# State and conversion words through PSUM, a first slice on VectorE, and a clip folded into a product, in a one-core attention and MLP kernel

## The chip, the cores and the metric

One NeuronCore of a Trainium2 chip runs the whole program. The metric is device time in microseconds (us). The time of a kernel is the median of its runs; one further execution was profiled, and it has a time of its own.

## The reference

For each of 4 batches and 8 heads a linear recurrence with complex decay runs over 768 steps (head width 48); its output goes through a 2D Fourier mix, a normalised MLP, a token mixer and a second MLP:

```python
scale = minimum(mag, 0.999) / (mag + 1e-06)       # mag = |a|
S_re, S_im = ar*S_re - ai*S_im + k v^T, ar*S_im + ai*S_re   # each step
y[t] = q[t] @ S_re
X = fft(fft(x, axis=1), axis=2); u = x + real(X)
un = (u - mean) / sqrt(var + 1e-06)
x = u + relu(un @ w_ch1) @ w_ch2                  # 384 -> 1536 -> 384
u = x + (relu(x^T @ w_tok1) @ w_tok2)^T           # 768 -> 256 -> 768
out = u + relu(u @ w3) @ w4
```

The inputs are float32, and so is the output. The weights arrive as 64-bit words.

## The kernel before, in words

Each batch has a chain part (VectorE, ScalarE, GpSimd, some TensorE) and a dense part (mostly TensorE). The chain of batch 0 runs alone; then the chain of batch b+1 runs beside the dense part of batch b, and the last batch's dense part runs with the one before it.

**The chain.** The 96-step chunks of all heads are scanned at once on 128 partitions: 49 steps, grouped in slices of 4 (batch 0, `first_scan`, L314) or of 3 (`scan`, L553). A slice is prepared by short stages: `st_b` (L357: Square on ScalarE, sum on GpSimd), `st_c` (L369: Ln, Exp, Square on ScalarE, a product on GpSimd), `st_d`, `st_e1`, `st_e2` (L379 to L401: limited magnitude, then the tile `A` of factors on VectorE and GpSimd). `st_f` (L403) does one step with three dependent VectorE instructions into the PSUM tile `P`. Beside each slice of `first_scan`, `st_s` squares the products and forms a reciprocal on ScalarE and GpSimd, `st_r` and `st_x` (L454, L458) scale the keys by it, `st_y` multiplies keys and queries, and `st_t` transposes them on TensorE. In `scan` the inverse length is a third row of `P`, limited to `R_CAP` at L625 once a slice.

`stage1` (L719) then walks over 8 chunks. `ch_u` (L788) forms keys times values on TensorE, adds the state `T` (L804), multiplies by gates (L810 to L812, the last of them on GpSimd) and writes the next `T` (L814); `ch_sc` masks the scores (L785) and `ch_y` forms the outputs. `stage2` (L986) does the Fourier mix and the normalisation.

**The conversions.** `convert` (L180) turns one block of 64-bit weights into a pair of float32 parts, 56 blocks in all, through a tile `cvt`: load, ScalarE `L191` (high words, scaled, absolute) and `L192` (low words), VectorE shift `L194`, GpSimd add `L196`, VectorE sign merge `L199`, ScalarE cast `L205`, GpSimd difference `L206`, store. Twenty blocks are converted during batch 0's chain (`tick`, `feed`); the other 36 (`lead`, L242) during batch 0's dense part, each shortly before its use, and ahead of the chain in VectorE's order.

**The dense part.** `mlp` (L939) runs groups of nine products per PSUM bank (L952, L974); ScalarE and VectorE split the hidden activations (L956, L965), and VectorE adds results (L977).

**Order.** Each instruction has a priority by stream (`RANK`, L60): TensorE takes the chain first, VectorE, ScalarE and GpSimd take dense work first, conversions second, chain third. A planner places the instructions of each engine in a fixed order from these priorities and its own estimates; `vq` in `first_scan` fixes VectorE's order by hand. PSUM has eight banks, handed out by `palloc` (L101) in rotation under three names: `s` 3, `l` 3, `p` 2.

Of the kernel before, what the change touches and what calls it, by code (L numbers as in the profile page):

```python
# [31 lines left out]
WC = (0, 0, 0, 0, 0, 0, 10, 12)  # L32
WZ, CL = 0, 1
XL = (0,), (0, 1, 2, 3, 4, 5)
# [19 lines left out]
def attn_fft_mixer_kernel(ctx: ExitStack, tc: tile.TileContext, aL, xL, vL, wL, qN, kN, vN, arN, aiN,  # L54
# [124 lines left out]

    def convert(p, j, w=None, held=True):  # L180

# [8 lines left out]
        lo, hi, a = raw[:, :, 0], raw[:, :, 1], t[:, 2 * n:3 * n]  # L190
        se.activation(out=a.bitcast(F32), in_=hi.bitcast(F32), func=ACTF.Abs, scale=2.0 ** -112)  # L191
# [25 lines left out]
    def begin():  # L217
        p, j = convs.pop(0)
        return convert(p, j, ws.place if (p, j) in early else None)

# [21 lines left out]
    def lead():  # L242

        keep, stream[0] = stream[0], BACK
        while len(begun) < 3 and later:
            p, j = later.pop(0)
            g = convert(p, j, ws.place, len(later) > 32)
# [66 lines left out]
    def first_scan(t, knd, qk):  # L314
# [42 lines left out]
        def st_b(i):  # L357
# [6 lines left out]
            if i >= AH:  # L364
                after(x, t[i - AH]["scan"])
            ge.tensor_tensor(out=tm[:, 0, :].rearrange("p (a c) -> p a c", c=48), in0=sq[:, :, 0, :], in1=sq[:, :, 1, :], op=ALU.add)  # L366
            d["tm"] = tm

        def st_c(i):  # L369
# [4 lines left out]

            se.activation(out=tt, in_=r0, func=ACTF.Square, accum_out=low[:, i:i + 1])
            ge.tensor_tensor(out=tt, in0=x, in1=tt, op=ALU.mult)

# [14 lines left out]
        def st_e2(i):  # L392
            d = t[i]
            n = d["n"]
            A = with_ap(alloc(turns("A", ("A", "T")), [128, 4, 192], name="A"), 0, [(192, n), (48, 4), (1, 48)])
            vq(ve.tensor_tensor(out=A[:, :, 2:4, :], in0=d["raw"], in1=d["c1"].unsqueeze(2).to_broadcast([128, n, 2, 48]), op=ALU.mult))
            ge.tensor_tensor(out=A[:, :, 0:2, :], in0=with_ap(A[:, 0, 3, :], 0, [(192, n), (0, 2), (1, 48)]),
                             in1=with_ap(both, 0, [(0, n), (1, 2), (0, 48)]), op=ALU.mult)
            d["A"] = A
            P = palloc("l" if i % 3 == 2 else "p", [128, N4, 96])  # L400
            d["P"] = P[:, 0:n, :].rearrange("p n (c f) -> p n c f", c=2)  # L401

        def st_f(i, j, between=()):  # L403
# [3 lines left out]
            if s == 0:  # L407
                se.copy(out=P[64:128, 0, 0, :], in_=A[64:128, 0, 2, :])
                se.copy(out=P[64:128, 0, 1, :], in_=A[64:128, 0, 1, :])
                ve.memset(P[0:64, 0, 0, :], 1.0)  # L410
                ve.memset(P[0:64, 0, 1, :], 0.0)
                for f in between:
                    f()
                return
# [99 lines left out]
        def line_up(i):  # L514
# [38 lines left out]
    def scan(b, t, knd, qk):  # L553
# [57 lines left out]
        def st_f(i, j):  # L611
# [20 lines left out]
        def st_g(i):  # L632
# [86 lines left out]
    def stage1(b):  # L719
# [68 lines left out]
        def ch_u(c):  # L788
            d = st[c]
            ps = palloc(PU, [112, 8, 48])  # L790
            for h in range(8):
                vv = d["v"][:, h * 48:h * 48 + 48]
                te.matmul(out=ps[0:64, h, :], lhsT=d["kt"][:, h, 0:64], rhs=vv)  # L793
                te.matmul(out=ps[64:112, h, :], lhsT=d["kt"][:, h, 64:112], rhs=vv)
            g = gm[b % 2].rearrange("p k (h c) -> p k h c", c=8)[:, :, :, c:c + 1]
# [16 lines left out]
            st["yop"] = (ge if c else ve).tensor_tensor(out=v8(y)[64:112], in0=a[0:48], in1=gb(1, 0, 48), op=ALU.mult)  # L812
            T = alloc("e", [112, 384], name="T")
# [566 lines left out]
```

## Time and profile before

| | |
|---|---|
| time, median of 3 runs (lowest, highest) | 1082.09 us (1080.92, 1084.59) |
| profiled execution: own time, span | 1079.18 us, 1077.4 us |
| TensorE, VectorE, ScalarE, GpSimd busy, share of the span | 91%, 72%, 48%, 39% |
| mean granted TensorE clock | 0.967 |

The span is the stretch that the trace covers; the execution's own time is 1.8 us more. An engine counts as busy while one of its instructions runs, also while that instruction is held up inside. A matmul that was issued behind another overlaps it, so the duration of one is longer than its spacing. PE is TensorE, DVE VectorE, ACT ScalarE, POOL GpSimd. A granted clock of 1.00 is 2.4 GHz.

### The profile page before, as it was taken

What the parts mean: (1) busy time and instruction counts of PE and PEld (TensorE: products, weight loads), DVE (VectorE), ACT (ScalarE), POOL (GpSimd) and SP (SyncE); (2) the same over time, 40 slices, a digit from 0 to 9 for tenths busy, and PEclk for the clock granted to TensorE, in tenths of its full rate; (3) what the DMA queues carried; (4) which work ended last, traced back from release to release, by engine and by line L of the source; (5) the groups of instructions that cost most, each with busy time, mean ns of one, the idle gap of its engine ahead of it and who ended that gap; (6) DMA issues with size and microseconds to landing.
All of it is one profiled execution on the core that took longest, in us unless ns stands there. A gap on an engine that the chain in (4) does not pass through costs nothing.

```text
span 1077.4 us, 21129 instructions
## 1 busy us (share of the span) xinstructions
PE 979.0 (91%) x7314; PEld 915.2 (85%) x7314; DVE 773.1 (72%) x2121; ACT 511.9 (48%) x1425; POOL 415.1 (39%) x553
## 2 busy tenths in 40 slices
PE   1568787989889999799998999999999999999997
PEld 0338765989789887699998899999889999999997
DVE  6988887989999779899758889874845433433332
ACT  7753445777876226877414667742243212221111
POOL 6635985573586455344336312423622002000000
PEclk9978896999999999899998999999999999999999
DMA  6238843786758646365664256755224434544522
GB/s 222 49 99 240 268 157 120 251 262 188 238 166 288 194 132 193 92 179 167 168 189 142 78 155 196 217 140 149 88 77 158 135 104 147 176 131 132 170 95 76
DMA packets 98337, 173.09 MB, mean 161 GB/s; under 512 B 10928, under 2 KB 57904, under 8 KB 97712
## 3 DMA queue, kind: packets, MB, share of 16 engines
q1 hardware_dynamic: 98224, 171.67, 51.8%
q8 instruction: 60, 0.98, 0.4%
q14 instruction: 53, 0.43, 0.1%
HBM read 132.31 MB, written 39.32 MB: 159 GB/s over the span
## 4 chain that ended last, share of the span: by engine, by line
PE 65%; DVE 18%; POOL 5%; issue 4%; DMA 4%; ACT 3%; SPq 0%; DVEq 0%; POOLq 0%; ACTq 0%
PE l L974 24%; PE l L952 23%; PE s L778 3%; PE s L655 2%; DMA cvt<-wL 2%; DVE cvt L199 2%; PE s L827 2%; POOL cvt L196 1%; PE s L1067 1%; PE s L1042 1%; POOL w L206 1%; PE s L833 1%; PE s L1181 1%; PE s L1199 1%; PE s L793 1%
## 5 line engine op out<-in xcount | busy, mean ns | idle before, releaser
L974 PE MATMUL l<-w,h 128*128 128x384 f32 x1728 | 326.1, 339 | 4.4 <-DVE h L965 2.9
L952 PE MATMUL l<-th,w 128*128 128x384 f32 x1152 | 316.3, 344 | 5.2 <-DVE h L965 4.2
L974 PEld LDWEIGHTS l<-w,h 128*128 128x128 f32 x1728 | 297.1, 188 | 8.8 <-DVE h L965 5.3
L952 PEld LDWEIGHTS l<-th,w 128*128 128x128 f32 x1152 | 212.5, 191 | 8.6 <-DVE h L965 6.3
L952 PE MATMUL l<-tl,w 128*128 128x384 f32 x576 | 196.1, 341 | 0.0
L956 ACT ACTIVATE h<-l 128x384 fp32r<-128x384 f32 x192 | 94.4, 492 | 211.9 <-PE l L952 211.4
L977 DVE TENSOR_TENSOR u<-u,l 128x384 f32<-128x384 f32 x192 | 105.2, 549 | 69.7 <-PE l L974 69.2
L965 DVE SCALAR_TENSOR_TENSOR h<-l,h 128x384 fp32r<-128x384 f32 x160 | 88.5, 554 | 89.6 <-ACT h L956 89.4
L952 PEld LDWEIGHTS l<-tl,w 128*128 128x128 f32 x576 | 110.0, 191 | 0.3 <-DVE tl L936 0.3
L196 POOL TENSOR_TENSOR cvt<-cvt 128x384 int32<-128x384 int32 x56 | 66.0, 1185 | 43.3 <-DVE cvt L194 10.4
L778 PE MATMUL s<-qkt 112*96 112x96 f32 x512 | 58.6, 263 | 9.9 <-DVE sc L785 9.9
L472 PE MATMUL s<-misc,y 128*112 128x128 f32 x96 | 22.4, 382 | 46.3 <-DVE y L450 24.1
L778 PEld LDWEIGHTS s<-qkt 112*96 112x96 f32 x512 | 52.5, 174 | 12.7 <-DVE sc L785 10.9
L472 PEld LDWEIGHTS s<-misc,y 128*112 128x112 f32 x96 | 14.7, 184 | 55.7 <-POOL tm L366 18.9
L1166 POOL TENSOR_TENSOR xl<-u,xh 128x384 fp32r<-128x384 f32 x18 | 18.1, 1013 | 105.8 <-ACT xh L1165 105.8
L206 POOL TENSOR_TENSOR w<-cvt,w 128x384 fp32r<-128x384 f32 x44 | 52.0, 1190 | 8.0 <-ACT w L205 7.7
L199 DVE SCALAR_TENSOR_TENSOR cvt<-cvt 128x384 int32<-128x384 int32 x56 | 45.3, 816 | 5.1 <-POOL cvt L196 4.9
L584 POOL TENSOR_TENSOR tm<-tm 128x144 f32<-128x144 f32 (+1 forms) x51 | 25.3, 497 | 58.9 <-ACT tm L583 58.5
L628 DVE TENSOR_TENSOR p<-p,A 128x144 f32<-128x144 f32 x144 | 44.8, 311 | 2.0
L655 PE MATMUL s<-misc,y 128*112 128x128 f32 x288 | 45.2, 276 | 0.9 <-DVE y L639 0.5
L811 POOL TENSOR_TENSOR yc<-Aa,gm 48x384 f32<-48x384 f32 x18 | 20.6, 1145 | 65.9 <-DVE Aa L804 65.6
L602 POOL TENSOR_TENSOR A<-raw,tm 128x144 f32<-128x144 f32 (+1 forms) x51 | 26.5, 519 | 47.4 <-DVE tm L600 28.5
(222 smaller groups left out, 1961.0 us busy)
## 6 DMA issues: line engine op xcount, KB each, us to landing
w<-wscr SPq DMA_DIRECT2D x180, 384.0 KB, 3.5
cvt<-wL SPq DMA_DIRECT2D x56, 384.0 KB, 4.9
wscr<-w SPq DMA_DIRECT2D x44, 384.0 KB, 3.6
Kn<-kn SPq DMA_DIRECT2D x56, 192.0 KB, 4.2
kn<-y SPq DMA_DIRECT2D x96, 96.0 KB, 2.4
raw<-aL SPq DMA_DIRECT2D x48, 144.0 KB, 3.2
xx<-xL SPq DMA_DIRECT2D x48, 144.0 KB, 3.0
V<-vL SPq DMA_DIRECT2D x32, 144.0 KB, 2.9
```

Of the source, the lines that this page charges most:

```text
L196: x = ge.tensor_tensor(out=a, in0=a, in1=lo, op=ALU.add)
L199: rest(ve.scalar_tensor_tensor(out=a, in0=hi, scalar=-0x80000000, in1=a, op0=ALU.bitwise_and, op1=ALU.bitwise_or))
L206: ge.tensor_tensor(out=parts[:, 1, :], in0=a.bitcast(F32), in1=r32(parts[:, 0, :]), op=ALU.subtract)
L472: te.transpose(ps[:, j, :], y[:, j, 0:112], ident)
L628: ve.tensor_tensor(out=cur, in0=prev, in1=A[:, j, 0:3, :], op=ALU.mult)
L655: te.transpose(ps[:, j, :], y[:, j, 0:112], ident)
L778: te.matmul(out=ps[:, j, :], lhsT=K[:, hc, :], rhs=Q[:, hc, :])
L952: te.matmul(out=ps, lhsT=w1[:, wi, kt * 128:kt * 128 + 128], rhs=x[g][:, kt, :], start=(n == 0), stop=(n == 8))
L956: x = se.activation(out=hi, in_=ps, func=ACTF.Relu)
L965: ve.scalar_tensor_tensor(out=lo, in0=ps, scalar=0.0, in1=r32(hi), op0=ALU.max, op1=ALU.subtract)
L974: te.matmul(out=ps, lhsT=hs[m][:, hi, tt * 128:tt * 128 + 128], rhs=w2[:, wi, :], start=(n == 0), stop=(n == 8))
L977: ve.tensor_tensor(out=u[tt], in0=u[tt], in1=ps, op=ALU.add)
```

## The change

PSUM gets a fourth name, `c`, with one bank, and `s` keeps two. Which banks a request for `s` may take depends on `lent`: 0 gives a rotation over s, s, c (three banks as before); 1, during the scan of batch 1, gives the two `s` banks; 2, from the end of that scan to the end of that pass, alternates `s` and `p`.

A conversion writes the scaled high words to a PSUM bank (`p`, or `c` for the later 36), keeps their sign there, and both VectorE instructions read them there. `first_scan` moves the three GpSimd instructions of slice 0 to VectorE, holds slice 1's Square until slice 0's last Square, sets up `P` earlier, copies slice 0's first factors on VectorE, moves the preparation of slice 1 into slice 0's steps, and writes the result of `st_r` to the PSUM tile `away`. `scan` drops L625 and limits inside the product with the keys. `ch_u` of batch 0 adds `T` by a product with the identity into the same PSUM bank, multiplies by the gate in place there, and does all gate products on VectorE.

```diff
-    PSB = {"s": 3, "l": 3, "p": 2}
+    PSB = {"s": 2, "l": 3, "p": 2, "c": 1}
+    lent, turn3 = [0], [0]
     def palloc(tag, shape):
+        if tag == "s":
+            turn3[0] += 1
+            tag = ("ssc", "s", "sp")[lent[0]]
+            tag = tag[turn3[0] % len(tag)]
...
     def convert(...):                       # far: 1 for the first 20, 2 for the later 36
+        if far:
+            x = palloc("p" if far == 1 else "c", [128, n])
+            se.activation(out=x, in_=hi.bitcast(F32), func=ACTF.Copy, scale=2.0 ** -112)
+            top = hi = x.bitcast(I32)
-        rest(ve.tensor_scalar(out=a, in0=a, scalar1=3, scalar2=None, op0=ALU.logical_shift_left))
+        rest(ve.tensor_scalar(out=a, in0=top, scalar1=3, scalar2=None, op0=ALU.logical_shift_left))
...
     # first_scan
+            if i == 1:
+                after(x, t[0]["lead"])      # lead: slice 0's Square in st_c
-            ge.tensor_tensor(...)           # st_b sum, st_c product, st_e2 product
+            if i: ge.tensor_tensor(...)
+            else: vq(ve.tensor_tensor(...))
...
-                se.copy(out=P[64:128, 0, 0, :], in_=A[64:128, 0, 2, :])
-                se.copy(out=P[64:128, 0, 1, :], in_=A[64:128, 0, 1, :])
+                vq(ve.tensor_copy(out=P[64:128, 0, 0, :], in_=A[64:128, 0, 2, :]))
+                vq(ve.tensor_copy(out=P[64:128, 0, 1, :], in_=A[64:128, 0, 1, :]))
...
+            o = with_ap(away[0], 192, [(48, t[i]["n"]), (1, 48)])
-            vq(ve.scalar_tensor_tensor(out=e[:, :, 0, :], in0=e[:, :, 0, :], scalar=-2.0, ...))
+            vq(ve.scalar_tensor_tensor(out=o, in0=e[:, :, 0, :], scalar=-2.0, ...))
-            vq(ve.scalar_tensor_tensor(out=x, in0=d["ss"][:, :, 0, :], scalar=-1.0, in1=x, ...))
+            vq(ve.scalar_tensor_tensor(out=x, in0=d["inv"], scalar=-1.0, in1=x, ...))
...
+                if not i:
+                    at = (5, 6, 7)          # slice 2's preparation, later
+                    fs[2] += [lambda: st_d(1)]
+                    fs[3] += [lambda: st_e1(1)]
+                    fs[4] += [lambda: st_e2(1)]
...
     # scan
-            if j == CL:
-                ve.tensor_scalar(out=prev[:, 2, :], in0=prev[:, 2, :], scalar1=R_CAP, scalar2=None, op0=ALU.min)
-            ve.tensor_tensor(out=xx[:, :, 1, :], in0=xx[:, :, 1, :], in1=P[:, 0:m, 2, :], op=ALU.mult)
+            ve.scalar_tensor_tensor(out=xx[:, :, 1, :], in0=P[:, 0:m, 2, :], scalar=R_CAP, in1=xx[:, :, 1, :], op0=ALU.min, op1=ALU.mult)
...
     # ch_u, batch 0 (b == 0)
-                ve.tensor_tensor(out=v8(a), in0=v8(st["T"]), in1=ps, op=ALU.add)
+                te.matmul(out=ps.rearrange("p h e -> p (h e)"), lhsT=ident[0:112, 0:112], rhs=st["T"], start=False, stop=True)
-            st["yop"] = (ge if c else ve).tensor_tensor(...)
+            st["yop"] = (ge if c and b else ve).tensor_tensor(...)
+            if not b:
+                x = a.rearrange("p h e -> p (h e)")
+                ve.tensor_tensor(out=a, in0=a, in1=gb(0, 0, 112), op=ALU.mult)
...
+        lent[0] *= 2                        # stage1, after the scan
+        lent[0] = int(not b)                # main loop, before the chain of batch b+1
```

## Rows read from the trace of the kernel before

**Rows 1.** Stretches: busy us (instructions) per engine, PEclk, DMA share, GB/s.

```profile
20.00:40.00 20.00, 8.09 (x31) 5.40 (x32) 19.86 (x75) 15.80 (x48) 13.50 (x20) 1.00 0.23 54
...
104.00:126.00 22.00, 15.13 (x222) 13.92 (x221) 19.02 (x31) 9.46 (x20) 21.69 (x15) 0.81 0.82 261
...
180.00:340.00 160.00, 149.09 (x847) 141.35 (x848) 148.76 (x430) 121.94 (x345) 98.06 (x130) 0.98 0.68 221
...
430.00:440.00 10.00, 4.67 (x23) 3.48 (x22) 9.30 (x47) 7.74 (x22) 2.79 (x6) 0.76 0.17 43
```

**Rows 2.** Timeline of the start: start us, us, engine, line, out<-in, idle before.

```profile
3.21 0.52 ACT L363 ACTIVATE tm<-raw 128x384 f32<-128x384 f32 x1 [1.20 <-DMA raw<-aL]
...
5.73 0.52 ACT L363 ACTIVATE tm<-raw 128x384 f32<-128x384 f32 x1 [0.75 <-DMA raw<-aL]
...
8.92 0.36 DVE L389 SCALAR_TENSOR_TENSOR tm<-tm 128x192 f32<-128x192 f32 x1 [0.43 <-ACT tm L383]
...
9.31 0.56 DVE L396 TENSOR_TENSOR A<-raw,tm 128x384 f32<-128x384 f32 x1
...
13.39 0.24 DVE L421 TENSOR_TENSOR l<-p,A 128x96 f32<-128x96 f32 x1
...
16.97 0.27 DVE L421 TENSOR_TENSOR l<-p,A 128x96 f32<-128x96 f32 x1 [0.56 <-ACT ss L436]
```

**Rows 3.** Groups by line and form, VectorE, 20 to 56 us: busy, mean ns.

```profile
L461 DVE SCALAR_TENSOR_TENSOR xx<-ss,xx 128x192 f32<-128x192 f32 x7 | 5.7, 809 | 0.0
```

**Rows 4.** Timeline inside the first scan.

```profile
20.77 0.94 POOL L397 TENSOR_TENSOR A<-A,both 128x384 f32<-128x384 f32 x1
...
21.11 0.81 DVE L461 SCALAR_TENSOR_TENSOR xx<-ss,xx 128x192 f32<-128x192 f32 x1
...
67.34 0.34 DVE L461 SCALAR_TENSOR_TENSOR xx<-ss,xx 128x192 f32<-128x192 f32 x1
```

**Rows 5.** Groups on VectorE, 104 to 126 us.

```profile
L811 DVE TENSOR_TENSOR yc<-Aa,gm 48x384 f32<-48x384 f32 x3 | 3.8, 1273 | 0.0
...
L785 DVE TENSOR_TENSOR sc<-s,misc 96x384 f32<-96x384 f32 x6 | 3.0, 542 | 0.0
...
L810 DVE TENSOR_TENSOR Xx<-Aa,gm 112x384 f32<-112x384 f32 x3 | 2.9, 977 | 0.0
...
L804 DVE TENSOR_TENSOR Aa<-T,l 112x384 f32<-112x384 f32 x3 | 1.6, 542 | 0.0
```

**Rows 6.** Groups on GpSimd, 104 to 126 us.

```profile
L206 POOL TENSOR_TENSOR w<-cvt,w 128x384 fp32r<-128x384 f32 x6 | 10.6, 1782 | 0.0
...
L812 POOL TENSOR_TENSOR yc<-Aa,gm 48x384 f32<-48x384 f32 x2 | 1.9, 938 | 0.2
```

**Rows 7.** Timeline, VectorE: first and last of the seven writes of the chunk state.

```profile
86.33 0.56 DVE L814 TENSOR_TENSOR T<-Xx,yc 112x384 f32<-112x384 f32 x1
...
128.95 1.18 DVE L814 TENSOR_TENSOR T<-Xx,yc 112x384 f32<-112x384 f32 x1
```

**Rows 8.** Timeline, TensorE: products of this width against the identity.

```profile
140.73 2.02 PE L309 MATMUL l<-qkt,misc 112*128 112x384 f32 x4 [0.80 <-DVE qkt L1016]
```

**Rows 9.** Groups on VectorE, 146 to 171 us.

```profile
L199 DVE SCALAR_TENSOR_TENSOR cvt<-cvt 128x384 int32<-128x384 int32 x8 | 10.6, 1357 | 3.7 <-POOL cvt L196 3.7
```

**Rows 10.** Groups on VectorE, 180 to 340 us.

```profile
L199 DVE SCALAR_TENSOR_TENSOR cvt<-cvt 128x384 int32<-128x384 int32 x31 | 23.5, 757 | 0.5 <-POOL cvt L196 0.3 <-issue 0.2
...
L194 DVE TENSOR_SCALAR cvt<-cvt 128x384 int32<-128x384 int32 x31 | 12.6, 410 | 2.6 <-ACT cvt L191 2.5
```

**Rows 11.** Timeline of a burst of conversions, first and last of six L191.

```profile
323.58 0.56 ACT L191 ACTIVATE cvt<-cvt 128x384 f32<-128x384 f32 x1 [0.47 <-DMA cvt<-wL]
...
328.76 0.57 ACT L191 ACTIVATE cvt<-cvt 128x384 f32<-128x384 f32 x1
...
332.18 1.04 DVE L199 SCALAR_TENSOR_TENSOR cvt<-cvt 128x384 int32<-128x384 int32 x1
...
337.06 0.57 ACT L191 ACTIVATE cvt<-cvt 128x384 f32<-128x384 f32 x1
```

More of the change, by code (lines that the diff above doesn't have):

```diff
@@ L32 @@
 WC = (0, 0, 0, 0, 0, 0, 10, 12)
-WZ, CL = 0, 1
+WZ = 0
 XL = (0,), (0, 1, 2, 3, 4, 5)
@@ L178, in rest, with convert @@
             after(x, rests[0])
-    def convert(p, j, w=None, held=True):
+    def convert(p, j, w=None, held=True, far=False):
         n = 384
@@ L218, in begin @@
         p, j = convs.pop(0)
-        return convert(p, j, ws.place if (p, j) in early else None)
+        return convert(p, j, ws.place if (p, j) in early else None, far=True)
     def feed(n):
@@ L246, in lead @@
             p, j = later.pop(0)
-            g = convert(p, j, ws.place, len(later) > 32)
+            g = convert(p, j, ws.place, len(later) > 32, far=2)
             for _ in range(4):
@@ L365, in st_b @@
                 after(x, t[i - AH]["scan"])
-            ge.tensor_tensor(out=tm[:, 0, :].rearrange("p (a c) -> p a c", c=48), in0=sq[:, :, 0, :], in1=sq[:, :, 1, :], op=ALU.add)
+            if i == 1:
+                after(x, t[0]["lead"])
+            o = tm[:, 0, :].rearrange("p (a c) -> p a c", c=48)
+            if i:
+                ge.tensor_tensor(out=o, in0=sq[:, :, 0, :], in1=sq[:, :, 1, :], op=ALU.add)
+            else:
+                vq(ve.tensor_tensor(out=o, in0=sq[:, :, 0, :], in1=sq[:, :, 1, :], op=ALU.add))
             d["tm"] = tm
@@ L373, in st_c @@
             se.activation(out=r0, in_=r0, func=ACTF.Exp, scale=-0.5)
-            se.activation(out=tt, in_=r0, func=ACTF.Square, accum_out=low[:, i:i + 1])
-            ge.tensor_tensor(out=tt, in0=x, in1=tt, op=ALU.mult)
+            t[i]["lead"] = se.activation(out=tt, in_=r0, func=ACTF.Square, accum_out=low[:, i:i + 1])
+            if i:
+                ge.tensor_tensor(out=tt, in0=x, in1=tt, op=ALU.mult)
+            else:
+                vq(ve.tensor_tensor(out=tt, in0=x, in1=tt, op=ALU.mult))
         def st_d(i):
@@ L395, in st_e2 @@
             A = with_ap(alloc(turns("A", ("A", "T")), [128, 4, 192], name="A"), 0, [(192, n), (48, 4), (1, 48)])
[L396 to L399, printed above, removed]
             P = palloc("l" if i % 3 == 2 else "p", [128, N4, 96])
             d["P"] = P[:, 0:n, :].rearrange("p n (c f) -> p n c f", c=2)
+            if not i:
+                for j in range(2):
+                    ve.memset(d["P"][0:64, 0, j, :], 1.0 - j)
+            vq(ve.tensor_tensor(out=A[:, :, 2:4, :], in0=d["raw"], in1=d["c1"].unsqueeze(2).to_broadcast([128, n, 2, 48]), op=ALU.mult))
+            args = dict(out=A[:, :, 0:2, :], in0=with_ap(A[:, 0, 3, :], 0, [(192, n), (0, 2), (1, 48)]),
+                        in1=with_ap(both, 0, [(0, n), (1, 2), (0, 48)]), op=ALU.mult)
+            if i:
+                ge.tensor_tensor(**args)
+            else:
+                vq(ve.tensor_tensor(**args))
+            d["A"] = A
         def st_f(i, j, between=()):
@@ L460, in st_x @@
             x = d["xx"][:, :, 1, :]
-            vq(ve.scalar_tensor_tensor(out=x, in0=d["ss"][:, :, 0, :], scalar=-1.0, in1=x, op0=ALU.mult, op1=ALU.mult))
+            vq(ve.scalar_tensor_tensor(out=x, in0=d["inv"], scalar=-1.0, in1=x, op0=ALU.mult, op1=ALU.mult))
         def st_t(i, k):
@@ L523, in line_up @@
             if i + 2 < NS:
-                fs[1] += [lambda: st_d(i + 2)]
-                fs[4] += [lambda: st_e1(i + 2)]
-                fs[5] += [lambda: st_e2(i + 2)]
+                at = (1, 4, 5)
+                if not i:
+                    at = (5, 6, 7)
+                    fs[2] += [lambda: st_d(1)]
+                    fs[3] += [lambda: st_e1(1)]
+                    fs[4] += [lambda: st_e2(1)]
+                fs[at[0]] += [lambda: st_d(i + 2)]
+                fs[at[1]] += [lambda: st_e1(i + 2)]
+                fs[at[2]] += [lambda: st_e2(i + 2)]
             return [lambda f=f: [g() for g in f] for f in fs]
@@ L530, in first_scan @@
             st_a(i)
+        for j in range(2):
+            ge.tensor_scalar(out=both[:, j:j + 1], in0=sgn, scalar1=(-1.0, 1.0)[j], scalar2=None, op0=ALU.mult)
         part1(0)
         part1(1)
-        for j in range(2):
-            ge.tensor_scalar(out=both[:, j:j + 1], in0=sgn, scalar1=(-1.0, 1.0)[j], scalar2=None, op0=ALU.mult)
         part2(0)
         part1(2)
-        part2(1)
         for i in range(NS):
@@ L792, in ch_u @@
                 vv = d["v"][:, h * 48:h * 48 + 48]
-                te.matmul(out=ps[0:64, h, :], lhsT=d["kt"][:, h, 0:64], rhs=vv)
-                te.matmul(out=ps[64:112, h, :], lhsT=d["kt"][:, h, 64:112], rhs=vv)
+                te.matmul(out=ps[0:64, h, :], lhsT=d["kt"][:, h, 0:64], rhs=vv, start=bool(b or not c or not h), stop=bool(b or not c))
+                te.matmul(out=ps[64:112, h, :], lhsT=d["kt"][:, h, 64:112], rhs=vv, start=bool(b or not c or not h), stop=bool(b or not c))
             g = gm[b % 2].rearrange("p k (h c) -> p k h c", c=8)[:, :, :, c:c + 1]
@@ L801, in v8 @@
                 return ap.rearrange("p (h e) -> p h e", e=48)
-            if c:
+            if c and b:
                 a = alloc("e", [112, 384], name="Aa")
@@ L807, in ch_u @@
                 a = ps
+                if c:
+                    te.matmul(out=ps.rearrange("p h e -> p (h e)"), lhsT=ident[0:112, 0:112], rhs=st["T"], start=False, stop=True)
             y = yc[c % 2]
-            x = alloc("e", [112, 384], name="Xx")
-            ve.tensor_tensor(out=v8(x), in0=a, in1=gb(0, 0, 112), op=ALU.mult)
+            if b:
+                x = alloc("e", [112, 384], name="Xx")
+                ve.tensor_tensor(out=v8(x), in0=a, in1=gb(0, 0, 112), op=ALU.mult)
             (ge if c and b else ve).tensor_tensor(out=v8(y)[0:48], in0=a[64:112], in1=gb(1, 64, 112), op=ALU.mult)
-            st["yop"] = (ge if c else ve).tensor_tensor(out=v8(y)[64:112], in0=a[0:48], in1=gb(1, 0, 48), op=ALU.mult)
+            st["yop"] = (ge if c and b else ve).tensor_tensor(out=v8(y)[64:112], in0=a[0:48], in1=gb(1, 0, 48), op=ALU.mult)
+            if not b:
+                x = a.rearrange("p h e -> p (h e)")
+                ve.tensor_tensor(out=a, in0=a, in1=gb(0, 0, 112), op=ALU.mult)
             T = alloc("e", [112, 384], name="T")
```

13 lines of the change are left out of this document (7 added, 6 removed).

## The prediction

> **What bounds the kernel now.** I read the page first (TensorE is busy most of the span, but not at its start), then the table of stretches, the chain of waits, and the timelines and groups of the stretches that the change touches. The reader should see three regimes.
>
> Up to about 180 us batch 0's chain runs alone, and TensorE waits. In the first scan VectorE has 19.86 busy us in 20, in the chunk stage 19.02 in 22, and there GpSimd has 21.69 in 22 [rows 1]. From 180 to 340 us TensorE is busy 149.09 of 160 us and VectorE 148.76 [rows 1]: batch 0's dense part, the late conversions and batch 1's chain share VectorE. At 430 us TensorE, busy 4.67 in 10, waits for the end of batch 1's chain [rows 1]. Later TensorE is full, and nothing that the change saves on other engines counts there. So what is saved before 180 us shortens the run one for one, and VectorE's work up to 430 us counts through that wait.
>
> Second view: the same instruction has two prices. L461 takes 0.34 us alone, and 0.81 when it begins inside GpSimd's L397 [rows 4]; its mean is 809 ns [rows 3]. Between 104 and 126 us, with GpSimd full, L811 takes 1273 ns and L810 977, both with two inputs in SBUF, while L785 and L804 (one input in PSUM, same width) stay at 542 [rows 5]. So an input in PSUM takes the instruction out of the quarrel with GpSimd. L206 on GpSimd shows the other side of it, 1782 ns there [rows 6]. The change does this to L461, L810, L811, L814 and L199.
>
> **Slice 0 on VectorE.** Before, data are there at 3.21 us and the first step starts at 13.39, slice 1's first step at 16.97 [rows 2]. After, the path is one Square (0.52), four ScalarE instructions of half that width (I take 0.44, between 0.52 and VectorE's 0.36 for the same elements), four VectorE instructions of 0.36, two of 0.56, and two small copies of at most 0.24 [rows 2]: 0.52 + 1.76 + 1.44 + 1.12 + 0.48 = 5.3 us, so the first step starts near 8.5, 4.9 earlier. Slice 1 cannot keep all of it. Its Square runs at 5.73 in either kernel [rows 2]; behind it come GpSimd's two sums (about 0.6 each, estimated from L397's 0.94 [rows 4] at half width) and its A product (0.94), five ScalarE and three VectorE instructions at the prices above, 2.1 + 2.3 + 1.3 = 5.7 us, and 0.5 for hand-overs: about 12, against 16.97. Its `st_d` now sits between two VectorE steps of slice 0, and if its input is late, those steps are queued behind it. I take -4.5; bounds -1.5 (only one hop gone) and -5.5.
>
> **The word in PSUM in the first scan.** Seven L461 between 20 and 56 us fall from 809 to 340 ns: 7 x 0.47 = 3.3 us, on an engine that has no idle time there; I take -3.5 for the whole scan. L456, just ahead, still has both inputs in SBUF and may meet L397 instead: bound 0. Ten slices would give -4.7. ScalarE at 15.80 of 20 [rows 1] stays below full in the shorter period.
>
> **The state in PSUM.** T is written at 86.33 and, six chunks later, at 128.95 [rows 7]: 7.1 us a chunk. After the change VectorE has per chunk two masks of 0.54, two gate products, the in-place product and T at 0.56 each (T's price with no quarrel [rows 7]), and for two conversions two shifts and two merges at 0.55: 1.08 + 2.24 + 2.2 = 5.5 us. L804 (0.54) goes, L812 (938 ns of GpSimd [rows 6]) comes as 0.56. New on the path is one product with the identity, T to TensorE and back; four of that width took 2.02 us [rows 8], 0.5 each, 1.0 at the lower of the two clocks. It waits behind whatever the chunk has queued on TensorE; masks and conversions fill VectorE meanwhile, and without that cover it costs some 1.2 us a chunk. I take 5.9 us a chunk, 6 x 1.2 = -7.2; bounds -2 (nothing covered, GpSimd's conversions late) and -9.5 (VectorE alone).
>
> The shift L194 reads PSUM after the change; no row shows that. I price it at L785's 0.54, against the 410 ns mean [rows 10] it has now. The Trainium skill (VectorE: DVE Perf Modes, "Why PSUM operands drop a tier") says that a float32 operation with a PSUM operand falls to one element a cycle, which speaks against this edit; by that rule the sum stays, and if the shift kept its price, the sum would be some 3 us better.
>
> **Conversions behind the mirrors, 146 to 171 us.** Eight merges take 1357 ns each [rows 9], 0.8 more than alone: 6.5 us of VectorE, in a stretch that GpSimd and VectorE share. Against it, eight blocks were staged ahead on ScalarE; now two `p` banks hold at most two. I take -3; bounds -6.5 and +4 (each pair waits out a full round).
>
> **The later 36 conversions, and batch 1's chain.** Merges fall from 757 to 550 ns, shifts rise from 410 to 550 [rows 10]: 36 x (0.21 - 0.14) = 2.5 us less, and sixteen clips less; the quarrel that remains is between SBUF instructions as before. It counts by the wait at 430 us. I take -3, bounds -8 and +20. The +20 is the one bank `c`: from L191 to the end of its merge a block holds it, 328.76 to 333.22, 4.5 us, while the burst around it starts a block every (337.06 - 323.58) / 5 = 2.7 us [rows 11]. Conversions go ahead of the chain, and eight weight tiles are filled in advance, so I expect the bursts to spread out and not to stall TensorE.
>
> The clips of batches 2 and 3, and two `s` banks instead of three in one scan: nothing, beside a full TensorE; if the two banks hold TensorE's transposes up, that is inside the +20.
>
> **Sum.** -4.5 - 3.5 - 7.2 - 3 - 3 = -21.2 on 1079.18 (the profiled execution) = 1058.0. The median of the runs is 2.9 us above that execution, so I predict 1061. What takes over: TensorE, earlier; it then needs the first weights earlier, but their conversions move with the chunk stage.
>
> **Rivals.**
> *The word stays queued.* The instructions get shorter, but the stages wait for ScalarE and GpSimd, which keep their work: slice 1 and the chunks at their low bounds. For it: GpSimd's 21.69 of 22. Against: L812 leaves GpSimd and its conversions are held up less. 1082.1 - 1.5 - 2 - 2 - 3 = 1074.
> *The lent bank chokes the conversions* (slower). Each of 36 blocks holds `c` for 4.5 us, 161 us in all, just about the stretch that they have; in bursts each comes 1.8 us later than the one before, and the weight that TensorE waits for is the last of the chain. It decides from 21 / 36 = 0.6 us of lateness per block that the tiles in advance do not swallow; at 0.8 the end is 1061 + 29 = 1090, at the full 1.8 far above. For it: the hold. Against: 0.5 of the hold was the quarrel on L199, and the planner knows of the bank.
> *PSUM does not help* (the change does not do what it says): L785 is cheap only by its place in time. Then slice 0 alone is won, and the product with the identity costs 6 x 1.2: 1082.1 - 4.5 + 7.2 = 1085. Against: six L785 and three L804, none late.
> *All bounds good*: -5.5 - 4.7 - 9.5 - 6.5 - 8 = -34: 1048.
>
> **Numbers.** Forecast 0.62 (its own range 1050 to 1072), stages wait 0.16, all good 0.10, bank 0.08, PSUM no help 0.04. The range 1045 to 1077 leaves out the two slow cases and little else. About 0.3% (3.2 us) is what a measurement of this kernel tells from no change. Faster: 0.62 + 0.16 + 0.10 = 0.88; the slow rivals hold 0.12, of which 0.05 near no change: same 0.05, slower 0.07.
>
> **What would show it.** First step near 8.5 us, slice 1's near 12; L461 at 0.34; T seven times in 42.6 - 7 us, each 0.56; L199 near 550 everywhere; the first dense product some 18 us earlier; the wait at 430 earlier and not longer. Wrong if L199 or L814 still shows a second price, if ScalarE's L191 waits for L199 in a row of blocks while TensorE waits for weights, or if the time won before 180 us is gone by 450.

## The result, and the profile after

| | before | after |
|---|---|---|
| time, median of 4 runs each (lowest, highest) | 1081.51 us (1078.98, 1084.59) | 1066.64 us (1064.30, 1067.39) |
| ratio, 95% interval | | 0.9861 (0.9834 to 0.9889) |
| profiled execution: own time, span | 1079.18, 1077.4 us | 1067.39, 1065.6 us |
| TensorE, VectorE, GpSimd busy | 979.0, 773.1, 415.1 us | 976.5, 750.0, 393.3 us |
| first dense product starts | 179.74 us | 179.66 us |
| first transposes behind the chains of batches 1, 2, 3 | 435.47, 621.75, 807.32 us | 418.96, 613.26, 795.76 us |

A dense product is one TensorE product of an MLP or of the token mixer, 384 columns wide.

The time came out inside the range, 5.6 us above the forecast. But the forecast had 18 of its 21 us won before 180 us, and nothing at all is won there: the first dense product starts where it did. The stretches of the kernel after (columns as in [rows 1], the last two stretches added):

```profile
20.00:40.00 20.00, 7.10 (x28) 4.38 (x27) 18.55 (x71) 14.96 (x44) 13.45 (x20) 1.00 0.21 48
104.00:126.00 22.00, 17.95 (x308) 15.57 (x305) 18.53 (x36) 10.85 (x23) 13.94 (x15) 1.00 1.00 296
180.00:340.00 160.00, 152.44 (x890) 145.07 (x890) 149.52 (x431) 118.59 (x345) 87.48 (x124) 0.98 0.69 221
430.00:440.00 10.00, 10.00 (x61) 9.96 (x61) 9.20 (x30) 5.35 (x17) 3.32 (x6) 1.00 0.62 195
420.00:460.00 40.00, 40.00 (x247) 39.65 (x246) 35.76 (x115) 28.05 (x85) 12.36 (x23) 1.00 0.59 185
760.00:840.00 80.00, 78.40 (x506) 73.75 (x505) 42.65 (x104) 26.40 (x64) 19.52 (x24) 1.00 0.34 109
```

The last two of the kernel before:

```profile
420.00:460.00 40.00, 33.60 (x187) 28.47 (x186) 35.34 (x138) 31.23 (x92) 15.39 (x29) 0.87 0.44 124
760.00:840.00 80.00, 78.72 (x583) 73.53 (x583) 47.47 (x107) 26.76 (x67) 26.94 (x29) 1.00 0.35 109
```

GpSimd fell from 21.69 to 13.94 of 22 us in the chunk stage, as meant. In the first scan VectorE is no longer full (18.55 of 20, from 19.86) and the scan is not shorter: VectorE waits instead. The gain stands at 420 to 460 us, where TensorE's idle 6.4 us are gone and its granted clock no longer falls to 0.87. Part of this goes again before: from 180 to 420 us the granted clock is 0.96 after and 0.99 before. From 460 us on TensorE is nearly full in both kernels.

What fills that hole is seen on TensorE. Before, with the transposes of batch 1 waiting for ScalarE (L1146, the normalisation), there is nothing else to run:

```profile
430.52 0.73 PE L1114 MATMUL s<-misc,xT 112*128 112x112 f32 x4
431.16 0.73 PE L1114 MATMUL s<-misc,qkt 112*128 112x112 f32 x4
435.47 1.54 PE L932 MATMUL s<-misc,qkt 128*128 128x128 f32 x6 [3.58 <-ACT qkt L1146]
438.76 1.54 PE L932 MATMUL s<-misc,qkt 128*128 128x128 f32 x6 [1.75 <-DVE A L604]
```

After, products of batch 0's second MLP (L989) stand around the same transposes (L969):

```profile
418.61 0.33 PE L989 MATMUL l<-tl,w 128*128 128x384 f32 x1
418.79 0.34 PE L989 MATMUL l<-th,w 128*128 128x384 f32 x1
418.96 0.49 PE L969 MATMUL s<-misc,qkt 128*128 128x128 f32 x3
419.21 0.42 PE L989 MATMUL l<-th,w 128*128 128x384 f32 x1
```

So the question for the runs: which part of the change keeps dense products in store until a chain ends, and why the stages before 180 us, with their cheaper instructions, gave nothing.

### The profile page after: what moved, and what is told of

Its sections match the earlier page's. It is cut to its first block, busy times and chain, and to the rows that moved or that the text cites. A ratio compares the mean times of both kernels' runs of the same rounds, so it can differ in the third digit from the quotient of the medians.

```text
span 1065.6 us, 21108 instructions
## 1 busy us (share of the span) xinstructions
PE 976.5 (92%) x7326; PEld 916.8 (86%) x7326; DVE 750.0 (70%) x2078; ACT 507.5 (48%) x1423; POOL 393.3 (37%) x544
## 4 chain that ended last, share of the span: by engine, by line
PE 61%; DVE 2%; POOL 1%; DMA 1%; issue 1%; ACT 1%; SPq 0%; POOLq 0%; ACTq 0%
PE l L1011 22%; PE l L989 22%; PE s L809 2%; PE s L685 1%; PE s L1079 1%; PE s L1104 1%; PE s L1218 1%; PE s L1236 1%; DVE qkt L1053 1%; PE s L864 1%; PE c L1104 1%; PE c L685 1%; PE l L1236 1%; DMA cvt<-wL 1%; PE s L1151 1%
## 5 line engine op out<-in xcount | busy, mean ns | idle before, releaser
L989 PE MATMUL l<-th,w 128*128 128x384 f32 x1152 | 313.9, 341 | 4.1 <-ACT th L972 2.2
L989 PEld LDWEIGHTS l<-th,w 128*128 128x128 f32 x1152 | 209.9, 189 | 6.4 <-ACT th L972 3.0
L989 PE MATMUL l<-tl,w 128*128 128x384 f32 x576 | 194.3, 337 | 0.0
L989 PEld LDWEIGHTS l<-tl,w 128*128 128x128 f32 x576 | 108.9, 189 | 0.2
L207 POOL TENSOR_TENSOR cvt<-cvt 128x384 int32<-128x384 int32 x56 | 58.9, 1056 | 28.3 <-DVE cvt L205 22.9
L217 POOL TENSOR_TENSOR w<-cvt,w 128x384 fp32r<-128x384 f32 x44 | 46.0, 1050 | 52.2 <-ACT w L216 45.1
L499 PE MATMUL s<-misc,y 128*112 128x128 f32 x64 | 14.9, 378 | 42.1 <-DMA fk<-cFk 19.5
L203 ACT ACTIVATE cvt<-cvt 128x384 int32<-128x384 uint32 x56 | 31.3, 559 | 44.0 <-DMA cvt<-wL 41.2
L499 PEld LDWEIGHTS s<-misc,y 128*112 128x112 f32 x64 | 9.6, 181 | 47.9 <-POOL ss L463 22.8
L1000 POOL TENSOR_TENSOR h<-full,h 128x384 fp32r<-128x384 f32 x32 | 33.0, 1030 | 39.0 <-ACT full L999 37.2
L660 DVE TENSOR_TENSOR p<-p,yt 128x96 f32<-128x96 f32 x144 | 37.5, 260 | 2.2
L809 PE MATMUL s<-qkt 112*96 112x96 f32 x328 | 38.6, 267 | 0.0
```

The source lines that it names most:

```text
L207: x = ge.tensor_tensor(out=a, in0=a, in1=lo, op=ALU.add)
L217: ge.tensor_tensor(out=parts[:, 1, :], in0=a.bitcast(F32), in1=r32(parts[:, 0, :]), op=ALU.subtract)
L660: ve.tensor_tensor(out=cur[:, 0:2, :], in0=cur[:, 0:2, :], in1=y, op=ALU.add)
L809: te.matmul(out=ps[:, j, :], lhsT=K[:, hc, :], rhs=Q[:, hc, :])
L989: te.matmul(out=ps, lhsT=w1[:, wi, kt * 128:kt * 128 + 128], rhs=x[g][:, kt, :], start=(n == 0), stop=(n == 8))
L1000: ge.tensor_tensor(out=lo, in0=full, in1=r32(hi), op=ALU.subtract)
```

## The experiments

In all runs below the ratio is to the kernel before on the same chip (medians there 1080.43, 1079.51 and 1080.05 us for the a, the b, and the c and d runs).

### One part at a time (a1 to a4)

Four kernels, each the kernel before with one part of the change. a1, the limit folded into the product:

```diff
-            if j == CL:
-                ve.tensor_scalar(out=prev[:, 2, :], in0=prev[:, 2, :], scalar1=R_CAP, scalar2=None, op0=ALU.min)
...
-            ve.tensor_tensor(out=xx[:, :, 1, :], in0=xx[:, :, 1, :], in1=P[:, 0:m, 2, :], op=ALU.mult)
+            ve.scalar_tensor_tensor(out=xx[:, :, 1, :], in0=P[:, 0:m, 2, :], scalar=R_CAP, in1=xx[:, :, 1, :], op0=ALU.min, op1=ALU.mult)
```

> The kernel before with one part of the change alone: the clip at L625 goes, and the limit stands inside the product with the keys. Theory 1 (the gain comes from VectorE's conversions in batch 1's stretch): sixteen instructions of about 0.2 us less in a scan that VectorE shares; batch 1's chain ends at most 3 us earlier, total 0 to -3 us. Rival (the clip sat on the dependent steps of the scan, and its going is the gain): -6 to -12 us, and the wait of TensorE at 430 us shrinks.

Measured: 1078.74 us, ratio 0.9990 (0.9972 to 1.0008). a2, the words through PSUM with the lent bank:

```diff
-    PSB = {"s": 3, "l": 3, "p": 2}
+    PSB = {"s": 2, "l": 3, "p": 2, "c": 1}
...
-            g = convert(p, j, ws.place, len(later) > 32)
+            g = convert(p, j, ws.place, len(later) > 32, far=2)
...
```

> The kernel before with the conversions' words through PSUM alone, and with it the banks: s 2, c 1, and the lending (2 banks for s in batch 1's scan, 4 behind it). Theory 1: this carries most of the gain, -7 to -14 us, all of it behind 180 us; L199's counterpart shows about 550 ns everywhere, and the transposes before batch 1's dense part, at 435.5 us before, start 8 to 15 us earlier. Rival (the clip or the state make the gain): -0 to -4 us. Rival (one bank for the conversions chokes them): slower than before.

Measured: 1084.81 us, ratio 1.0036 (1.0016 to 1.0057): slower by 0.4%, where theory 1 had a gain. The transposes behind batch 1's chain do come earlier (419.27 us), and the one bank does not choke the conversions: TensorE's idle time from 180 to 420 us is 14.4 us against 15.4 before. a3, the hunks of `first_scan` alone:

```diff
-            ge.tensor_tensor(out=tm[:, 0, :].rearrange("p (a c) -> p a c", c=48), in0=sq[:, :, 0, :], in1=sq[:, :, 1, :], op=ALU.add)
+            if i == 1:
+                after(x, t[0]["lead"])
...
+            o = with_ap(away[0], 192, [(48, t[i]["n"]), (1, 48)])
...
```

> The kernel before with the first scan's part alone (slice 0 on VectorE, slice 1's preparation inside slice 0's steps, the result of st_r in PSUM). Theory 1, from the trace of the changed kernel: first step some 3 us earlier, slice 1's not earlier, period of a slice 5.1 to 5.3 us as before, because each slice's first step waits for ScalarE's Square of the PSUM bank that it reads; scan's end 0 to 3 us later, total 0 to +3 us. The prediction on record: -8 us.

Measured: 1079.62 us, ratio 0.9999 (0.9981 to 1.0016). a4, the hunks of `ch_u` alone:

```diff
...
+                if c:
+                    te.matmul(out=ps.rearrange("p h e -> p (h e)"), lhsT=ident[0:112, 0:112], rhs=st["T"], start=False, stop=True)
...
+                ve.tensor_tensor(out=a, in0=a, in1=gb(0, 0, 112), op=ALU.mult)
...
```

> The kernel before with the state through PSUM alone (batch 0's chunks). Theory 1: seven writes of T in 38 to 40 us against 42.6, T at 0.56 us each, but the first dense product at 179.7 us moves by less than 2 us, because the conversions behind the mirrors set it: total -2 to +1 us. The prediction on record: -7 us, the first dense product 7 us earlier.

Measured: 1074.36 us, ratio 0.9960 (0.9934 to 0.9987): here the recorded -7 was near, and theory 1 missed. The four differences from 1080.43 are -1.7, +4.4, -0.8 and -6.1, about -4 together, against -14.9 of the whole: the parts are not additive. a2's trace shows why its gain turns round. It has no hole at 420 us, and a new one at 800 (stretches, then TensorE in that stretch):

```profile
420.00:460.00 40.00, 39.70 (x240) 38.62 (x239) 34.05 (x116) 28.80 (x83) 14.98 (x24) 1.00 0.60 187
760.00:840.00 80.00, 69.03 (x445) 59.47 (x444) 42.09 (x96) 21.72 (x55) 22.98 (x26) 0.74 0.21 66
```

```profile
812.56 0.87 PE L944 MATMUL s<-misc,qkt 128*128 128x128 f32 x3 [0.64 <-ACT rs L1148]
819.09 0.90 PE L944 MATMUL c<-misc,qkt 128*128 128x128 f32 x3 [5.66 <-ACT qkt L1158]
819.79 0.85 PE L944 MATMUL s<-misc,qkt 128*128 128x128 f32 x3
822.14 0.90 PE L944 MATMUL s<-misc,qkt 128*128 128x128 f32 x3 [1.50 <-ACT qkt L1158]
```

The dense work that does not need batch 3's transposes is through before they can start; TensorE idles 11.0 us and the mean granted clock of the stretch is 0.74. That is the same kind of hole as before's at 431 us, at batch 3's chain and not at batch 1's.

### Two parts together (b4), and the start of the scan (b1 to b3)

b4 is a2 and a1 together (both diffs above).

> The kernel before with two parts of the change only: the conversions through PSUM with the lent bank, and the later scans' limit folded into the product. Alone they measured +4 us (1084.81) and -2 us (1078.74) against 1080.43. Theory (they need each other: the words bring batch 1's chain forward and the clip's removal lets batches 2 and 3's chains follow, so TensorE does not run out of dense work near 800 us): transposes behind batch 3's chain near 795 to 800 (811 with the words alone), TensorE idle below 4 us in 760 to 840 (11.0 with the words alone), time 1067 to 1073. Rival (parts add up): +2 us, 1081 to 1084, and the whole's gain lies in another pair, state with one of the others.

Measured: 1064.82 us, ratio 0.9853 (0.9812 to 0.9895). It is faster than either expectation and as fast as the whole change, without the first scan's part and without the state in PSUM. Its stretch at the end of batch 3's chain:

```profile
760.00:840.00 80.00, 78.40 (x485) 73.83 (x484) 40.74 (x100) 27.13 (x64) 17.23 (x21) 1.00 0.34 114
```

b1 to b3 start from the kernel after and try to mend the first scan. b1 puts the Squares of slices 2 and 3 behind the Copies (L403) of slices 0 and 1 in ScalarE's order:

```diff
+            if i in (2, 3):
+                after(x, t[i - 2]["mag"])
...
-                    fs[3] += [lambda: st_e1(1)]
+                    fs[3] += [lambda: st_e1(1), lambda: part1(3)]
...
```

> The kernel after, with ScalarE's order at the start changed: slices 2 and 3's Squares stand behind the Copies of the magnitudes of slices 0 and 1, so those Copies no longer stand behind a Square that waits for a transfer. Theory (ScalarE's order holds slice 0's first step at 10.40 us and slice 1's at 17.39): first step near 8.5 to 9.5, slice 1's near 13 to 15.5, last step of the scan (75.01) 1 to 2 us earlier, first dense product (179.66) 1 to 2 us earlier; time 1064 to 1067. Rival (the start is slack, the scan's period of 5.25 us per pair of slices and the chunk stage set the end): the first steps move, the last step and the time do not, 1066 to 1068.

Measured: 1064.95 us, ratio 0.9849 (0.9807 to 0.9891). First step at 9.37 us, slice 1's at 14.97, the scan's last at 72.86 (75.01 after), first dense product at 170.90 (179.66 after). The steps moved about as the theory had it, the first dense product by far more; of its 8.8 us the span keeps 2.0. Slice 1's first step in b1:

```profile
14.97 0.27 DVE L448 TENSOR_TENSOR l<-p,A 128x96 f32<-128x96 f32 x1 [0.47 <-ACT ss L463]
```

b2 issues the Square of a slice's product inside the next slice's first step:

```diff
+            if 0 < i < NS:
+                fs[0] += [lambda: st_s(i - 1)]
...
-            st_s(i)
+            if i == NS - 1:
+                st_s(i)
```

> The kernel after, with one ScalarE instruction of the scan moved: the Square of the previous slice's product, which reads the PSUM bank that the next slice's first step reads too, is issued inside that first step and not ahead of it. Theory (the wait of 0.30 us of each first step for ScalarE's Square, with the Square itself, is what took the place of the queued word): the first step follows its product about 0.3 to 0.8 us sooner, but the Square's result is wanted by the slice's own sum, so 0.2 to 0.5 us per slice is left; 14 slices give 3 to 7 us at the last step of the scan (75.01 to 68 to 72) and about as much at the first dense product (179.66 to 173 to 177); time 1060 to 1065. Rival (the period is set by the Square's result, and the wait only moves behind it): last step within 1 us of 75.0, time 1066 to 1068.

Measured: 1081.91 us, ratio 1.0023 (0.9995 to 1.0051), and the last step of the scan at 80.42, 5.4 us later than without the edit: both theories missed. b2's VectorE, then its ScalarE, show it:

```profile
38.75 0.24 DVE L449 TENSOR_TENSOR yt<-p,A 128x96 f32<-128x96 f32 x1
39.69 0.97 DVE L482 SCALAR_TENSOR_TENSOR l<-ss 128x192 f32<-128x192 f32 x1 [0.70 <-POOL ss L466]
...
45.92 0.98 DVE L482 SCALAR_TENSOR_TENSOR l<-ss 128x192 f32<-128x192 f32 x1 [0.70 <-POOL ss L466]
```

```profile
41.71 0.49 ACT L461 ACTIVATE ss<-p 128x384 f32<-128x384 f32 x1 [2.31 <-DVE yt L449]
```

The Square now waits for the step, its result comes later through ScalarE and GpSimd, L482 waits for that and then meets GpSimd (0.97 us). Two L482, one per slice, are 6.23 us apart here, against 5.25 in the kernel after. In the order of the kernel after the first step waits for the Square, which costs less.

b3 has both edits.

> The kernel after with both edits of ScalarE's order: the Squares of slices 2 and 3 behind the Copies of slices 0 and 1, and the Square of the previous product inside the next slice's first step. Theory: the two gains add, last step of the scan at 67 to 71 us, first dense product 172 to 176, time 1058 to 1064, below both kernels. Rival (what is won before 180 us is lost again where TensorE runs out of dense work near 800 us): first dense product earlier by 4 us or more, time 1065 to 1069.

Measured: 1084.80 us, ratio 1.0062 (1.0037 to 1.0087); missed for b2's reason. TensorE also idles 11.4 (b2) and 11.3 us (b3) from 760 to 840 us, the hole of a2, although both keep the folded limit.

### Why the two need each other (c1, d1 to d3)

c1 is the kernel after with the first scan of the kernel before (a3's hunks undone).

> The kernel after with the first scan of the kernel before; TensorE's order of instructions is the same but for two rows. Theory (the first scan's part of the change brings nothing, since its last step moved from 72.35 to 75.01 us): last step near 72.4, first dense product at 173 to 177 us against 179.66, time 1061 to 1066, not above the 1064.8 of the words and the folded limit by more than 2 us. Rival (the prediction's: this part is worth 8 us by itself and the rest of the gain hides a loss): 1070 to 1075.

Measured: 1058.65 us, ratio 0.9823 (0.9792 to 0.9854), the fastest of all and faster than its theory; its interval overlaps that of the change itself. First dense product at 172.73, last step of the scan at 73.28. d1 is b4 with the limit kept as an instruction of its own in batch 1:

```diff
+            if j == CL and b == 1:
+                ve.tensor_scalar(out=prev[:, 2, :], in0=prev[:, 2, :], scalar1=R_CAP, scalar2=None, op0=ALU.min)
...
```

> The kernel before with the conversions through PSUM and the lent bank, and with the limit folded into the product in batches 2 and 3 only; batch 1's scan keeps its sixteen clips. With all 48 clips it measured 1084.8, with none 1064.8. Theory (VectorE, busy 85 to 96 percent in the later scans, sets when batch 3's chain ends, and TensorE has run out of dense work by then, so each clip of each batch counts): a third of the clips back, the last xT of batch 3 at 761 to 767 us (776.13 with all, 759.61 with none), time 1066 to 1074. Rival, as the prediction had it (the clips of batches 2 and 3 lie beside a full TensorE and count nothing): as with all clips, 1083 to 1086.

Measured: 1077.24 us, ratio 0.9971 (0.9950 to 0.9991), last xT of batch 3 at 770.52: between the two expectations. d2 is b4 with one VectorE instruction more per slice, whose result nothing reads:

```diff
...
+            ve.tensor_scalar(out=junk, in0=P[:, 0, 2, :], scalar1=R_CAP, scalar2=None, op0=ALU.min)
```

> The words with the folded limit (1064.8), and 48 VectorE instructions more, one per slice of batches 1 to 3: each has the clip's form and size (0.21 us, 48 words of each of 128 partitions, from PSUM) but writes to a place that nothing reads, so no step waits for it. Theory (it is VectorE's time that the clips cost, 10 us in all): the last xT of batch 3 at 770 to 777 us, time 1078 to 1087. Rival (it is the clip's place as a link between two steps of the scan): 1064 to 1068.

Measured: 1080.72 us, ratio 1.0013 (0.9989 to 1.0036), last xT at 770.60: as the theory of VectorE's time had it. The clips of the kernel before, and then d2's stand-ins, whose 9.5 us (48 x 198 ns) brought back some 16 us:

```profile
L625 DVE TENSOR_SCALAR p<-p x48: 192/216/217, 190.7 to 711.7; 128x48 f32<-128x48 f32 x48
```

```profile
L651 DVE TENSOR_SCALAR junk<-p x48: 191/198/202, 190.6 to 710.8; 128x48 f32<-128x48 f32 x48
```

d3 is the kernel after without the words' part (a2's hunks undone).

> The kernel after without the words part: conversions and banks as in the kernel before; the first scan, the state in PSUM and the folded limit stay. Theory (without the words batch 1's chain ends late again, TensorE waits near 430 us as before, and the rest cannot make that good): first transposes behind batch 1's chain at 428 to 434 us (418.96 after, 435.47 before), TensorE idle 4 us or more in 420 to 460, time 1071 to 1078. Rival (any change that comes with the folded limit gives the gain): 1064 to 1068.

Measured: 1072.66 us, ratio 0.9937 (0.9915 to 0.9959), transposes behind batch 1's chain at 427.60, TensorE idle 4.2 us in 420 to 460: as the theory had it, but for 0.4 us at the transposes.

That 9.5 us of VectorE bring back 16 and d1's 3.3 (16 x 0.206) bring back 12 is no price per instruction; it is a step. Its place is in TensorE's fixed order, counted in the instructions of each kernel: how many dense products (of width 384; a batch has 936, two MLPs of 432 and 72 between them) stand ahead of the first transposes behind a chain, beside TensorE's idle time there (stretch less busy):

| kernels | products ahead, chains 1, 2, 3 | idle 420 to 460, 760 to 840 us | medians, us |
|---|---|---|---|
| before, a3, a4 | 936, 1556, 2256 | 6.4 to 8.1, 1.3 | 1081.5, 1079.6, 1074.4 |
| a1, d3 | 930, 1500, 2233 | 4.2 to 4.4, 0 to 2.2 | 1078.7, 1072.7 |
| a2, b2, b3, d1, d2 | 873 to 891, 1608 to 1656, 2304 | 0 to 0.3, 9.3 to 11.4 | 1077.2 to 1084.8 |
| after, b1, b4, c1 | 842 to 855, 1584, 2266 or 2267 | 0, 1.6 | 1058.7 to 1066.6 |

Both numbers have a ceiling. At chain 1 it is 936, all of batch 0: the kernel before puts every product of batch 0 ahead of those transposes (a1 and d3 all but 6) and has none left for the wait. At chain 3 it is 2304, two batches and the first MLP of batch 2 (2 x 936 + 432); in the code the rest follows on the last batch's transposes. All five kernels of the third row stand at it. The last row alone stays under both. a2's hunks give the first: with them 45 (a2) to 94 (b1) products are held back at chain 1. These hunks hold the words and the lent banks together, and no run separates the two. By themselves they let the dense work run ahead into the second ceiling; with the folded limit, on a VectorE that is busy 134.86 of 140 us in batch 1's scan (190 to 330 us), the chains end sooner (batch 3's last xT at 759.61 us in b4, 776.13 in a2) and the order stays 37 products under it (2304 - 2267). But the order also tips on small edits elsewhere: b2 touches batch 0's scan alone and falls into the third row. So d1 and d2 show that 3 to 10 us of VectorE suffice to tip it, and b2 that something else does too; how much of the 15 us is VectorE's time and how much the luck of the order stays open. The order is the planner's, made from its own estimates, and no run sets it by hand: that the step sits there is read from counts that go with the idle times in all fourteen kernels, and is not tested by itself.

## Why the prediction was right, and where it was not

**The sum came out by other terms.** Of -21.2, some -18 were to stand before 180 us (0 measured) and -3 later (-12 of span measured). The direction and the size were right; the places were not, so that the total agrees within 5.6 us is luck.

**Slice 0 on VectorE (-4.5).** First step at 10.40, not 8.5; slice 1's at 17.39, not 12. The step that failed is the sum over ScalarE's instructions, which left out what stands between them in its order. ScalarE, then VectorE:

```profile
7.23 0.52 ACT L374 ACTIVATE tm<-raw 128x384 f32<-128x384 f32 x1 [0.93 <-DMA raw<-aL]
7.66 0.35 ACT L403 ACTIVATE tm<-tm 128x192 f32<-128x192 f32 x1
...
11.43 0.52 ACT L374 ACTIVATE tm<-raw 128x384 f32<-128x384 f32 x1 [2.00 <-DMA raw<-aL]
...
13.22 0.35 ACT L403 ACTIVATE tm<-tm 128x192 f32<-128x192 f32 x1
```

```profile
10.40 0.27 DVE L446 TENSOR_TENSOR l<-p,A 128x96 f32<-128x96 f32 x1
...
13.60 0.45 DVE L409 SCALAR_TENSOR_TENSOR tm<-tm 128x192 f32<-128x192 f32 x1 [2.33 <-ACT tm L403]
```

Each L403 that VectorE waits for stands behind a Square of a later slice, and that Square waits for its transfer. b1 takes the Squares out of the way and gets 1.03 and 2.42 us of it back.

**The word in PSUM in the first scan (-3.5).** L461's successor L488 does fall to its price alone, but the scan ends 2.66 us later. VectorE from 20 to 72 us, before and then after (busy, mean ns, idle just before):

```profile
L461 DVE SCALAR_TENSOR_TENSOR xx<-ss,xx 128x192 f32<-128x192 f32 x11 | 7.0, 640 | 0.0
L421 DVE TENSOR_TENSOR l<-p,A 128x96 f32<-128x96 f32 x26 | 6.8, 260 | 0.8 <-ACT ss L436 0.6
```

```profile
L446 DVE TENSOR_TENSOR l<-p,A 128x96 f32<-128x96 f32 x26 | 6.8, 262 | 2.3 <-ACT ss L461 2.1
L488 DVE SCALAR_TENSOR_TENSOR xx<-l,xx 128x192 f32<-128x192 f32 x10 | 3.5, 347 | 0.0
```

3.5 us of work go (3.2 for the same eleven slices), and the first step of each slice waits 2.0 us longer in all (the two groups over `l` and `p` differ by 1.5 and 0.5) for ScalarE's Square of the product before it, in the bank that the step reads; L482 (527 against L456's 492 ns) and L402 (410 against L382's 349) take over some of the quarrel. In the middle of the scan a slice takes 5.25 us, where it took 5.12. Before, the long L461 lay in the shadow of that wait: where it takes 0.81 us the next first step follows at once, and where it takes 0.34 the same 0.30 us of waiting appear, in the kernel before itself:

```profile
46.72 0.81 DVE L461 SCALAR_TENSOR_TENSOR xx<-ss,xx 128x192 f32<-128x192 f32 x1
47.45 0.25 DVE L421 TENSOR_TENSOR l<-p,A 128x96 f32<-128x96 f32 x1
...
57.40 0.34 DVE L461 SCALAR_TENSOR_TENSOR xx<-ss,xx 128x192 f32<-128x192 f32 x1
58.05 0.27 DVE L421 TENSOR_TENSOR l<-l,A 128x96 f32<-128x96 f32 x1 [0.30 <-ACT ss L436]
```

"An engine that has no idle time" was near the truth, but part of its busy time was a wait in disguise. The Trainium skill (PSUM — Partial Sum Buffer, "PSUM bank collisions raise a hardware error") says that two engines must not touch one bank in the same partitions at once, reads included; the trace agrees that the two reads are kept apart, at 0.30 us of idle per slice in one order, and b2 shows that the other order costs more.

**The state in PSUM (-7.2).** Alone it was right: a4's T is written at 86.34 and 122.32, 36.0 us against 42.6, -6.6; its first dense product comes 6.0 us earlier and half of that reaches the end of the span (1074.3). Beside the words it is half as much. After, VectorE with one row of TensorE:

```profile
90.69 0.56 DVE L851 TENSOR_TENSOR T<-l,yc 112x384 f32<-112x384 f32 x1
...
94.88 1.51 PE L840 MATMUL l<-T,misc 112*112 112x384 f32 x2
...
96.43 0.56 DVE L845 TENSOR_TENSOR yc<-l,gm 48x384 f32<-48x384 f32 x1 [3.33 <-PE l L840]
...
129.73 0.56 DVE L851 TENSOR_TENSOR T<-l,yc 112x384 f32<-112x384 f32 x1
```

39.0 us, and the first T 4.4 us later than before: 2.7 from the scan, the rest with the words (a2 and b4, whose scan ends as before's, write it 1.7 and 1.2 us later). The prediction's cover failed at the start, 3.33 us and 0.71 at the next chunk: the product with the identity stands behind the chunk's products on TensorE, whose granted clock is 0.56 from 87 to 100 us (0.90 in a4). Its price was too low as well: it runs as two instructions, 0.90 us together at a granted clock of 1.00 (100.38) and 1.51 at 0.50 (94.88), where the sum had 0.5 and 1.0. The four of [rows 8] ran at a mean granted clock of 0.72, so they are not the price at the upper one.

**Conversions behind the mirrors (-3).** The merge has one price now, 548 ns here (140 to 175 us) and from 180 to 340 us, against 1357 and 757 in [rows 9, 10]; the shift rises to 549 as priced (VectorE, 180 to 340 us):

```profile
L205 DVE TENSOR_SCALAR cvt<-c 128x384 int32<-128x384 int32 x28 | 15.4, 549 | 2.0 <-ACT c L198 1.8
L210 DVE SCALAR_TENSOR_TENSOR cvt<-c,cvt 128x384 int32<-128x384 int32 x27 | 14.8, 548 | 0.3 <-POOL cvt L207 0.2
```

But VectorE did not set that stretch (it is busy 19.66 of 30 us from 130 to 160). There the profiled executions of c1 and after differ most, with the same order on TensorE but for a few small products. After, and then c1, TensorE:

```profile
140.40 3.24 PE L320 MATMUL l<-qkt,misc 112*128 112x96 f32 x6
143.57 1.55 PE L1079 MATMUL s<-dcos,qkt 112*63 112x97 f32 x8
145.06 1.00 PE L320 MATMUL l<-qkt,misc 112*128 112x190 f32 x2
145.85 1.86 PE L1079 MATMUL s<-dcos,qkt 112*128 112x97 f32 x8
```

```profile
137.89 1.71 PE L320 MATMUL l<-qkt,misc 112*128 112x96 f32 x6
139.53 0.88 PE L1058 MATMUL s<-dcos,qkt 112*63 112x97 f32 x8
140.34 0.59 PE L320 MATMUL l<-qkt,misc 112*128 112x190 f32 x2
140.77 1.03 PE L1058 MATMUL s<-dcos,qkt 112*128 112x97 f32 x8
```

The granted clock is 0.50 from 140 to 145 us after and 1.00 in c1 (half, 1.2 GHz, against 2.4): these four groups take 7.3 us against 3.9. In the 2.5 us ahead of them TensorE had been busy for 1.20 after and for 1.87 in c1. c1's first dense product comes 6.9 us earlier than after's (172.73). That the first scan's part costs the change something is not shown by this: there is one trace of each, the intervals overlap, and c1's own runs differ with the clock. Four of them, at a mean granted clock of 0.975 to 0.978, took 1056.8 to 1058.7 us; the two at 0.970 and 0.968 took 1062.1 and 1065.8, as the change's four at 0.968 to 0.972 took 1064.3 to 1067.4.

**The later conversions and batch 1's chain (-3, bounds -8 and +20).** The bank did little harm. From 180 to 420 us ScalarE's L198 waits 12 times for the merge of an earlier block (L210), 9.8 us in all and 2.6 at most, but TensorE waits for a weight (L216) only 1.9 us in all, and its idle time went from 15.4 to 13.0 us. This term was mis-sized; it is where the gain is, -6.4 us of idle at 420 to 460 and the clock of 0.87. (In the prediction's aside on the shift, 36 x 0.14 is 5.0 us, not some 3.)

**The clips of batches 2 and 3: nothing, beside a full TensorE.** This is the step that was wrong in kind. Idle time of a full TensorE was read as cover for the chains, but the chains then set whether it stays full: with all clips kept the words lose 4 us (a2), with none they win 15 (b4). "What is saved before 180 us shortens the run one for one" fell too: of b1's 8.8 us the span kept 2.0, of a4's 6.0 it kept 3.1.

## What to carry to other kernels

Where one engine carries a backlog that fills the waits of another chain, ask at every end of a chain how much backlog is left in the fixed order: a part that brings the backlog forward is worth nothing, or less, until the chains are shortened too, so such parts are tested together as well as alone. An instruction that got longer in a quarrel is worth its excess only if nothing else was being waited for at the same time. And in an engine's queue, what stands ahead of the instruction that others wait for counts, most of all if it waits for a transfer.

## What the runs showed of the hardware

The same eight products of 112x97 took 1.55 us at a granted clock of 0.50 and 0.88 at 1.00, in stretches where the order was the same and VectorE's and GpSimd's work ahead of them differed by a few microseconds; these four groups, with TensorE on the path, took 7.3 or 3.9 us. On VectorE, instructions with an input in PSUM kept one price beside GpSimd everywhere (in the kernel after, no group's longest is over 5% above its median; T seven times 557 to 558 ns, where [rows 7] had 560 and 1180).
